# LSH attention feeding a domain mixture of experts: the softmax division moves behind the product with v

## The chip, the core and the metric

The kernel runs on one core of one Trainium2 chip. The metric is device microseconds (us) of one execution; three runs of the kernel before gave 774.47, 777.2 and 779.48 us, median 777.2.

The engines are named as the profile names them: PE (TensorE, matmuls and transposes; PEld is its weight load), DVE (VectorE), ACT (ScalarE), POOL (GpSimd) and SP, whose queue issues every DMA of this program. Each engine works through its own instructions in order; an instruction whose inputs are not there holds up all that stand behind it on that engine, and the same holds for the DMA issues in SP's queue.

## The reference

Two batches of eight heads, 768 positions, head size 64, everything in float32. Queries and keys are hashed by the signs of six projections; a query attends to the keys of its own bucket alone. The result, head by head side by side, goes through four experts weighted by given probabilities.

```
mask   = q_bucket[:, :, :, None] == k_bucket[:, :, None, :]
scores = where(mask, q @ k.T / sqrt(64), -1e9)
attn   = exp(scores - max(scores))
attn   = attn / (sum(attn) + 1e-9)
x      = attn @ v                      # (1536, 512) after heads are laid side by side
out    = sum over e of p[:, e] * (relu(x @ w1[e]) @ w2[e])   # w1 512x1024, w2 1024x512
```

## The kernel before, in words

float32 products are made of float32r parts: each operand is split into a rounded part and a remainder, and three products (high x high, high x low, low x high) are added up in PSUM. That is why so many tiles come as pairs: `pthi` and `ptlo`, `hh` and `hl`, `xhi` and `xlo`, `w1hi` and `w1lo`.

**Attention** is a loop over steps, one step for each tile of 128 queries: 2 x 8 heads x 6 tiles. Two tiles are a pair, in the code a group `g`. A tile goes through these stages, each some steps behind the first:

- S: scores on PE into `sps` (L337, L339), then on DVE the row minimum of the negated scores, copied out to `p` (L344).
- E: exp on ACT, in place, with the row sum in `den` (L360).
- M and N: on DVE `den` + 1e-9 (L493) and the reciprocal `rd` (L367); then POOL multiplies `p` by it, 128x768 for each tile (L370).
- T, for heads 0 to 8 of 16: PE transposes `p` into `ptps` (L386), ACT copies the rounded part to `pthi` (L390), DVE subtracts for `ptlo` (L391).
- X and H, for the seven last heads, which the code calls light: DVE transposes 32x32 blocks of `p` into `t` (L403); SP writes `t` to DRAM as `scr` (L407) and, when that has landed, reads it back in another order as `px` in four DMAs (L410). Two steps later ACT makes `pthi` of `px` (L424) and POOL `ptlo` (L425). There is one `px` buffer.
- V: PE multiplies with `vv`, first the `pthi` part, one step later the `ptlo` part (`pv`, L435); ACT and DVE add the two halves into `xf` (L452, L457, L464), and after an odd head POOL makes `xhi` and `xlo` of it (L468, L471).
- P: once a head, in its first three steps, the preparation of the next head: PE transposes, ACT and DVE split into `ah` and `al`, SP copies parts between partitions (`q<-ah` twice, `k<-ah`, then `ah<-al`), PE and ACT compute the hash signs, POOL turns them into mask rows (`al`, L279), SP copies those (`k<-al`, L287). The next head's second score matmul (L339) reads them. SP also loads q and k (`tqk`) and v (`tv`) for the head after the next.

The order of all this is written out by hand: in each step the stages are issued in the order of the string `ORDER`, and the constants `LAG_...` say how many steps after S a stage comes. An engine's instruction order is this issue order.

**Experts**: 16 units of 512 hidden columns (8 for each batch). A unit does 8 groups of 12 matmuls into a PSUM tile `mps` (L602 to L604), each followed by a relu `hh` on ACT (L609) and a remainder `hl` on DVE (L610), then 6 groups of 12 matmuls (L625 to L627), added into `acc` on DVE (L635). `mps`, `ptps` and `pv` share four PSUM buffers. The weights are loaded as `ws` (L566) and split on DVE and POOL (L577, L578).

Attention of batch 0 runs first. Then the experts of batch 0 run, with steps of attention of batch 1 put between their matmuls by a running count of estimated PE time, and last the experts of batch 1 alone.

Of the kernel before, what the change touches and what calls it, by code (L numbers as in the profile page):

```python
# [8 lines left out]
F32 = mybir.dt.float32  # L9
F32R = mybir.dt.float32r  # L10
ACTF = mybir.ActivationFunctionType
ALU = mybir.AluOpType
PSUM = bass.MemoryType.PSUM

P = 128
# [3 lines left out]
SGN_SCALE = float(2**20)  # L19
ATT_PACE = 1.04  # L20
LAG_E = 1
LAG_N = 2
LAG_T = 6
LAG_V = 7
PP_BUFS = 5
TW = 3
QK_AT = 1
XADD_POOL = 0
# [3 lines left out]
N_WARM = 16  # L32
WARM = (2, 4)
FIRST = 2
SPLIT_N = 1
W_STEP = 24
PREP_AT = 0
ORDER = "MTNXVSEP"
LIGHT_FROM = 9
LAG_VL = 8  # L40
DRAIN = 1000
LAG_X = 4
LAG_H = 6


@with_exitstack
def tile_lsh_attention__then__domain_moe(
# [11 lines left out]
    nc = tc.nc  # L59
    B, H, S, D = q.shape  # L60
    NB = proj.shape[1]
    E, DM, F = w1.shape
    NT = S // P
# [7 lines left out]
    G = 2  # L71
    GN = G * P
# [7 lines left out]
    const = ctx.enter_context(tc.tile_pool(name="const", bufs=1))  # L80
# [5 lines left out]
    dr = ctx.enter_context(tc.tile_pool(name="dr", bufs=2, space=bass.MemoryType.DRAM))  # L86
    ptp = ctx.enter_context(tc.tile_pool(name="ptp", bufs=2))
    sm = ctx.enter_context(tc.tile_pool(name="sm", bufs=6))
    xs = ctx.enter_context(tc.tile_pool(name="xs", bufs=2))
# [41 lines left out]
    def setup():  # L131
        nc.sync.dma_start(out=pr[0:D], in_=proj)
        nc.sync.dma_start(out=pr[D:P], in_=proj)
        nc.vector.memset(warm, 0.0)
        nc.scalar.activation(warm[:, 0:1], warm[:, 0:1], ACTF.Exp)
        make_identity(nc, ident)
        keep_warm(N_WARM)
        step_column(qk_scale, ((0, -scale), (D, 1.0)))
        step_column(
            sgn_bias, ((0, -TINY), (MQ + NB, TINY), (MQE, 0.0), (MK, TINY), (MK + NB, -TINY), (MKE, 0.0))  # L140
        )
        step_column(bit_mul, ((0, 0.5), (MK, BIG / 2)))
        nc.vector.memset(phi.bitcast(F32), 0.0)
        nc.vector.memset(plo.bitcast(F32), 0.0)
        for rows, m, sign in ((slice(0, D), MQ, -1.0), (slice(D, P), MK, -1.0)):
            sg = sign if m == MQ else sign
            for i, s in ((0, sg), (1, -sg)):
                cols = slice(m + i * NB, m + (i + 1) * NB)
                nc.vector.tensor_scalar(out=phi[rows, cols], in0=pr[rows], scalar1=s, scalar2=None, op0=ALU.mult)
                nc.vector.scalar_tensor_tensor(  # L150
                    out=plo[rows, cols],
                    in0=pr[rows],
                    scalar=s,
                    in1=phi[rows, cols].bitcast(F32),
                    op0=ALU.mult,
                    op1=ALU.subtract,
                )
# [152 lines left out]

    probs_t = {}
    dens = {}
    rds = {}
    pts = {}
    pvs = {}
    xf = {}
# [38 lines left out]
    def stage_e(b, h, t):  # L355
        pt, nb = probs_t[b, h, t]
        g, o = divmod(t, G)
        if o == 0:
            dens[b, h, g] = sm.tile([P, G], F32, tag="den", name="den")
        nc.scalar.activation(pt, pt, ACTF.Exp, bias=nb, scale=-1.0, accum_out=dens[b, h, g][:, o : o + 1])  # L360

    def stage_n(b, h, g):
        den = dens.pop((b, h, g))
        rd = sm.tile([P, G], F32, tag="rd", name="rd")
        if not SPLIT_N:
            nc.vector.tensor_scalar(out=den, in0=den, scalar1=1e-9, scalar2=None, op0=ALU.add)
        nc.vector.reciprocal(out=rd, in_=den)  # L367
        for o in range(G):
            pt, _ = probs_t[b, h, g * G + o]
            nc.gpsimd.tensor_scalar(  # L370
                out=pt, in0=pt, scalar1=rd[:, o : o + 1], scalar2=1.0, op0=ALU.mult, op1=ALU.mult
            )

    def stage_t(b, h, t):
        pt, _ = probs_t.pop((b, h, t))
# [53 lines left out]
    def stage_v(b, h, g, part):  # L429
# [16 lines left out]
        j, odd = divmod(h, 2)  # L446
        if not odd:
            xf[b, j, g] = xs.tile([P, GN], F32, tag=f"xf{g}", name="xf", bufs=1)
        x = xf[b, j, g]
# [6 lines left out]
        elif light(b, h):  # L456
            nc.vector.tensor_tensor(  # L457
                out=x[mine].rearrange("p (t a q) -> p a t q", t=G, q=32),
                in0=ps[mine, :GN].rearrange("p (a t q) -> p a t q", t=G, q=32),
                in1=tmp[mine].rearrange("p (a t q) -> p a t q", t=G, q=32),  # L460
                op=ALU.add,
# [2 lines left out]
            nc.vector.tensor_tensor(out=x[mine], in0=ps[mine, :GN], in1=tmp[mine], op=ALU.add)  # L464
        if odd:
            x = xf.pop((b, j, g))
            sl = slice(g * GN, (g + 1) * GN)
            nc.gpsimd.tensor_scalar(  # L468
                out=xhi[b, j][:, sl], in0=x, scalar1=1.0, scalar2=1.0, op0=ALU.mult, op1=ALU.mult
            )  # L470
            nc.gpsimd.tensor_tensor(  # L471
                out=xlo[b, j][:, sl], in0=x, in1=xhi[b, j][:, sl].bitcast(F32), op=ALU.subtract
            )
# [5 lines left out]
    def attention():  # L479
# [3 lines left out]
        def do(op, i):  # L483
            if op == "N":
                j = i - LAG_N
                if 0 <= j < n and j % G == G - 1:
                    b, h, t = seq[j]
                    stage_n(b, h, t // G)
            elif op == "M":
                j = i - LAG_N  # L490
                if SPLIT_N and 0 <= j < n and j % G == G - 1:
                    den = dens[seq[j][0], seq[j][1], seq[j][2] // G]
                    nc.vector.tensor_scalar(out=den, in0=den, scalar1=1e-9, scalar2=None, op0=ALU.add)  # L493
            elif op == "T":
                j = i - LAG_T
                if 0 <= j < n and not light(*seq[j][:2]):
# [219 lines left out]
```

## Time and profile before

| | |
|---|---|
| runs | 774.47, 777.2, 779.48 us |
| profiled execution, first to last instruction (span) | 779.2 us; the run of 779.48 us is the one that fits it, 0.3 us around the span |
| busy | PE 752.8 us (97%), DVE 459.4 (59%), POOL 401.8 (52%), ACT 279.0 (36%) |
| mean granted TensorE clock | 0.987 of full speed |
| chain that ended last | PE 69%, DMA 10%, DVE 8%, POOL 6%, ACT 3% |

Busy time is that of modelled matmul ends, so PE at 97% is not PE at its peak. The shares are means over stages that differ: in the page's 40 slices DVE and ACT are at nine tenths until about 140 us and at three or less behind 480 us. The chain that ended last holds, besides PE, the DMA `px<-scr` (4%), the DMA `scr<-t` (3%) and POOL's `ptlo` (3%).

### The profile page before, as it was taken

What the parts mean: (1) busy time and instruction counts of PE and PEld (TensorE: products, weight loads), DVE (VectorE), ACT (ScalarE), POOL (GpSimd) and SP (SyncE); (2) the same over time, 40 slices, a digit from 0 to 9 for tenths busy, and PEclk for the clock granted to TensorE, in tenths of its full rate; (3) what the DMA queues carried; (4) which work ended last, traced back from release to release, by engine and by line L of the source; (5) the groups of instructions that cost most, each with busy time, mean ns of one, the idle gap of its engine ahead of it and who ended that gap; (6) DMA issues with size and microseconds to landing.
All of it is one profiled execution on the core that took longest, in us unless ns stands there. A gap on an engine that the chain in (4) does not pass through costs nothing.

```text
span 779.2 us, 11435 instructions
## 1 busy us (share of the span) xinstructions
PE 752.8 (97%) x4186; PEld 690.4 (89%) x4186; DVE 459.4 (59%) x876; ACT 279.0 (36%) x556; POOL 401.8 (52%) x381
## 2 busy tenths in 40 slices
PE   7899999999989899999989989999999999999998
PEld 6789989898979888999888889898989989899896
DVE  4899999946758478565766734343443434524342
ACT  4899989641343433426244131110201102011020
POOL 1656686724579668667796855132251322414220
PEclk8999999999999999999999999999999999999999
DMA  3544535334657877676565733231121211113002
GB/s 91 144 111 110 117 85 131 74 87 140 181 154 199 226 186 217 177 202 179 156 209 162 200 111 95 80 124 55 55 81 37 100 51 59 55 54 109 28 27 82
DMA packets 67344, 92.29 MB, mean 118 GB/s; under 512 B 29860, under 2 KB 42660, under 8 KB 67288
## 3 DMA queue, kind: packets, MB, share of 16 engines
q1 hardware_dynamic: 67288, 91.56, 42.0%
q8 instruction: 33, 0.54, 0.3%
q14 instruction: 23, 0.19, 0.1%
HBM read 59.53 MB, written 19.66 MB: 102 GB/s over the span
## 4 chain that ended last, share of the span: by engine, by line
PE 69%; DMA 10%; DVE 8%; POOL 6%; ACT 3%; issue 2%; SPq 2%; POOLq 0%; ACTq 0%; DVEq 0%
PE mps L625 9%; PE mps L626 9%; PE mps L627 9%; PE mps L602 9%; PE mps L603 9%; PE mps L604 9%; PE pv L435 5%; DMA px<-scr 4%; DMA scr<-t 3%; PE ptps L386 3%; POOL ptlo L425 3%; PE sps L339 2%; PE sps L337 2%; DVE p L344 2%; DMA ah<-al 2%
## 5 line engine op out<-in xcount | busy, mean ns | idle before, releaser
L602 PE MATMUL mps<-xhi,w1hi 128*128 128x384 f32 x512 | 173.5, 339 | 5.8 <-DVE hl L610 5.8
L578 POOL TENSOR_TENSOR w1lo<-ws,w1hi 128x512 fp32r<-128x512 f32 x64 | 83.1, 1302 | 178.3 <-DVE w1hi L577 155.3
L604 PE MATMUL mps<-xhi,w1lo 128*128 128x384 f32 x512 | 172.9, 338 | 0.0
L603 PE MATMUL mps<-xlo,w1hi 128*128 128x384 f32 x512 | 172.9, 338 | 0.0
L609 ACT ACTIVATE hh<-mps 128x384 fp32r<-128x384 f32 x128 | 61.9, 490 | 301.1 <-PE mps L604 301.0
L610 DVE SCALAR_TENSOR_TENSOR hl<-mps,hh 128x384 fp32r<-128x384 f32 x128 | 70.4, 555 | 143.1 <-ACT hh L609 142.9
L625 PE MATMUL mps<-w2hi,hh 128*128 128x512 f32 x384 | 151.6, 395 | 0.4 <-DVE hl L610 0.4
L626 PE MATMUL mps<-w2lo,hh 128*128 128x512 f32 x384 | 150.9, 393 | 0.0
L627 PE MATMUL mps<-w2hi,hl 128*128 128x512 f32 x384 | 150.6, 392 | 0.0
L635 DVE SCALAR_TENSOR_TENSOR acc<-mps,pe,acc 128x512 f32<-128x512 f32 x84 | 62.9, 748 | 118.0 <-PE mps L627 118.0
L578 POOL TENSOR_TENSOR w2lo<-ws,w2hi 128x512 fp32r<-128x512 f32 x64 | 86.5, 1380 | 46.0 <-issue 37.8
L370 POOL TENSOR_SCALAR p<-p,rd 128x768 f32<-128x768 f32 x96 | 87.6, 924 | 32.1 <-DVE rd L367 28.6
L602 PEld LDWEIGHTS mps<-xhi,w1hi 128*128 128x128 f32 x512 | 97.0, 189 | 7.1 <-DVE hl L610 6.6
L603 PEld LDWEIGHTS mps<-xlo,w1hi 128*128 128x128 f32 x512 | 97.0, 189 | 0.4
L604 PEld LDWEIGHTS mps<-xhi,w1lo 128*128 128x128 f32 x512 | 97.2, 190 | 0.0
L344 DVE TENSOR_SCALAR_CACHE_REDUCE p<-sps 128x768 f32<-128x768 f32 x96 | 90.8, 947 | 4.6 <-PE sps L339 3.3
L360 ACT ACTIVATE p<-p,nb 128x768 f32<-128x768 f32 x96 | 89.6, 933 | 9.4 <-DVE p L344 8.2
L425 POOL TENSOR_TENSOR ptlo<-px,pthi 128x768 fp32r<-128x768 f32 x42 | 77.1, 1858 | 25.6 <-ACT pthi L424 21.4
L627 PEld LDWEIGHTS mps<-w2hi,hl 128*128 128x128 f32 x384 | 72.8, 190 | 15.7
L625 PEld LDWEIGHTS mps<-w2hi,hh 128*128 128x128 f32 x384 | 72.7, 189 | 14.6 <-DVE hl L610 0.6
L626 PEld LDWEIGHTS mps<-w2lo,hh 128*128 128x128 f32 x384 | 72.8, 190 | 13.8
L424 ACT ACTIVATE pthi<-px 128x768 fp32r<-128x768 f32 x42 | 33.2, 838 | 109.9 <-DMA px<-scr 109.9
(82 smaller groups left out, 953.2 us busy)
## 6 DMA issues: line engine op xcount, KB each, us to landing
ws<-in_moe_w_dram SPq DMA_DIRECT2D x64, 512.0 KB, 3.3
scr<-t SPq DMA_DIRECT2D x21, 768.0 KB, 4.3
px<-scr SPq DMA_DIRECT2D x84, 192.0 KB, 3.9
q<-ah SPq DMA_DIRECT2D x30, 192.0 KB, 3.2
tv<-in_v_dram SPq DMA_DIRECT2D x16, 192.0 KB, 3.6
out_dram<-acc SPq DMA_DIRECT2D x12, 256.0 KB, 2.5
tqk<-in_q_dram SPq DMA_DIRECT2D x15, 192.0 KB, 4.2
tqk<-in_k_dram SPq DMA_DIRECT2D x15, 192.0 KB, 3.8
```

Of the source, the lines that this page charges most:

```text
L344: nc.vector.tensor_scalar(out=two(pt), in0=ps[:, :, :NH], scalar1=MASKED, scalar2=MASKED, op0=ALU.min, op1=ALU.min, accum_out=nb,)
L360: nc.scalar.activation(pt, pt, ACTF.Exp, bias=nb, scale=-1.0, accum_out=dens[b, h, g][:, o : o + 1])
L370: nc.gpsimd.tensor_scalar(out=pt, in0=pt, scalar1=rd[:, o : o + 1], scalar2=1.0, op0=ALU.mult, op1=ALU.mult)
L425: nc.gpsimd.tensor_tensor(out=fl[:, sl], in0=px[:, sl], in1=fh[:, sl].bitcast(F32), op=ALU.subtract)
L578: nc.gpsimd.tensor_tensor(out=lo[:, c + o], in0=t[:, o], in1=hi[:, c + o].bitcast(F32), op=ALU.subtract)
L602: nc.tensor.matmul(ps[:, :SB], w1hi[:, kk, fs], xhi[b, kk][:, sl], start=kk == 0, stop=False)
L603: nc.tensor.matmul(ps[:, :SB], w1hi[:, kk, fs], xlo[b, kk][:, sl], start=False, stop=False)
L604: nc.tensor.matmul(ps[:, :SB], w1lo[:, kk, fs], xhi[b, kk][:, sl], start=False, stop=kk == KD - 1)
L610: nc.vector.scalar_tensor_tensor(out=hl, in0=ps[:, :SB], scalar=0.0, in1=hh.bitcast(F32), op0=ALU.max, op1=ALU.subtract)
L625: nc.tensor.matmul(ps, hh[:, ts], w2hi[:, f], start=f == 0, stop=False)
L626: nc.tensor.matmul(ps, hh[:, ts], w2lo[:, f], start=False, stop=False)
L627: nc.tensor.matmul(ps, hl[:, ts], w2hi[:, f], start=False, stop=f == FC - 1)
```

## The change

The probabilities are no longer divided before the product with v. The rows of x are, behind it:

- Gone: the epsilon add on DVE (L493, stage M) and POOL's two products of 128x768 a pair (L370).
- The epsilon is added on ACT (an Identity with a bias of 1e-9, 128x2, behind the second exp of a pair).
- Stage N: DVE takes the reciprocal into two columns of a standing tile of 128x32, and transposes that tile in 32x32 blocks into `rt`. SP writes two DMAs of 4x32 from it, one for each tile, to a small DRAM row `row` of 2x128.
- A new stage R, one step later: SP reads `row` back, broadcast over the 64 partitions of the head's half, into `rdb`.
- When both heads of a pair of heads are in `xf`, POOL multiplies it by `rdb`, 128x256, ahead of `xhi` and `xlo`.
- All lags are shorter: T from 6 to 4 steps, V from 7 to 6 (light heads 8 to 7), X from 4 to 3, H from 6 to 5; N goes from 2 to 3. There are four `p` buffers in place of five. The order within a step is `TXVSENRP` in place of `MTNXVSEP`. Because the lags change by odd numbers, X, H and N now fall into the even steps, in which the preparation issues `q<-ah`, `k<-ah` or `k<-al`; before they fell into the odd ones, with `ah<-al` and the loads of q and k.

```diff
-LAG_N = 2
-LAG_T = 6
-LAG_V = 7
-PP_BUFS = 5
+LAG_N = 3
+LAG_R = 4
+LAG_T = 4
+LAG_V = 6
+PP_BUFS = 4
...
-ORDER = "MTNXVSEP"
+ORDER = "TXVSENRP"
 LIGHT_FROM = 9
-LAG_VL = 8
+LAG_VL = 7
 DRAIN = 1000
-LAG_X = 4
-LAG_H = 6
+LAG_X = 3
+LAG_H = 5
...
-    rds = {}
+    rds = [const.tile([P, 32], F32, name=f"rd{i}") for i in range(2)]
+    for t in rds:
+        nc.vector.memset(t, 1.0)
...
         nc.scalar.activation(pt, pt, ACTF.Exp, bias=nb, scale=-1.0, accum_out=dens[b, h, g][:, o : o + 1])
+        if o == G - 1:
+            den = dens[b, h, g]
+            nc.scalar.activation(den, den, ACTF.Identity, bias=eps)
...
     def stage_n(b, h, g):
         den = dens.pop((b, h, g))
-        rd = sm.tile([P, G], F32, tag="rd", name="rd")
-        if not SPLIT_N:
-            nc.vector.tensor_scalar(out=den, in0=den, scalar1=1e-9, scalar2=None, op0=ALU.add)
-        nc.vector.reciprocal(out=rd, in_=den)
+        rd = rds[(h * NT // G + g) % 2]
+        nc.vector.reciprocal(out=rd[:, 0:G], in_=den)
+        rt = sm.tile([P, 32], F32, tag="rt", name="rt", bufs=2)
+        nc.vector.transpose(out=rt, in_=rd)
+        rows[b, h, g] = dr.tile([G, P], F32, tag="row", name="row", bufs=6)
         for o in range(G):
-            pt, _ = probs_t[b, h, g * G + o]
-            nc.gpsimd.tensor_scalar(
-                out=pt, in0=pt, scalar1=rd[:, o : o + 1], scalar2=1.0, op0=ALU.mult, op1=ALU.mult
-            )
+            nc.sync.dma_start(out=rows[b, h, g][o].rearrange("(r q) -> r q", q=32), in_=rt[o:P:32])
+
+    def stage_r(b, h, g):
+        j, odd = divmod(h, 2)
+        if not odd:
+            rdbs[b, j, g] = xs.tile([P, GN], F32, tag=f"rdb{g}", name="rdb", bufs=1)
+        row = rows.pop((b, h, g))
+        nc.sync.dma_start(
+            out=rdbs[b, j, g][odd * D : (odd + 1) * D],
+            in_=row.rearrange("g p -> (g p)").partition_broadcast(D),
+        )
...
         if odd:
             x = xf.pop((b, j, g))
+            nc.gpsimd.tensor_tensor(out=x, in0=x, in1=rdbs.pop((b, j, g)), op=ALU.mult)
```

How the instructions stand, first SP's queue in the attention of batch 0, the issues of one head before (names are out<-in; the brackets list the semaphores waited for, DMAHW being earlier DMAs):

```order
L265 DMA q_1081<-ah 64x768 [waits Activation_49]
L266 DMA q_1081<-ah 64x768
L267 DMA k_1084<-ah 64x768 [waits DMAHW0_49,PE_49]
L274 DMA ah<-al 64x768 [waits DMAHW6_49,DMAHW1_49,DMAHW7_49,DVE_49,PE_49]
L180 DMA tqk<-in_q_dram 128x6x64 [waits DMAHW2_49]
L180 DMA tqk<-in_k_dram 128x6x64 [waits DMAHW3_49]
L287 DMA k_1084<-al 12x768 [waits DMAHW4_49,Pool_49]
L187 DMA tv<-in_v_dram 128x384 [waits DMAHW5_49,Pool_49]
```

These eight are all there is. The same place of the change, from the first preparation DMA of a head to its third pair of `row` writes:

```order
L267 DMA q_915<-ah 64x768 [waits DMAHW5_49,Activation_49]
L268 DMA q_915<-ah 64x768 [waits DMAHW6_49]
L269 DMA k_918<-ah 64x768 [waits PE_49]
L387 DMA rdb<-row 64x256 [waits DMAHW4_49,DMAHW3_49]
L276 DMA ah<-al 64x768 [waits DMAHW5_49,DMAHW1_49,DMAHW6_49,DVE_49,PE_49]
L182 DMA tqk<-in_q_dram 128x6x64 [waits DMAHW2_49]
L182 DMA tqk<-in_k_dram 128x6x64
L380 DMA row<-rt 4x32 [waits DVE_49]
L380 DMA row<-rt 4x32
L289 DMA k_918<-al 12x768 [waits Pool_49]
L387 DMA rdb<-row 64x256 [waits DMAHW7_49,DMAHW5_49,DMAHW4_49]
L380 DMA row<-rt 4x32 [waits DVE_49]
```

Between each pair of `row` writes and the `rdb` that waits for both stand the preparation's issues of that even step: three, one, and one (`tv`).

Next, SP's queue beside the experts, where a light head is in work. Before, from the end of one `px` to the next pair's:

```order
L410 DMA px<-scr 32x4x384 [waits DMAHW5_49]
L274 DMA ah<-al 64x768 [waits DMAHW6_49,PE_49]
L180 DMA tqk<-in_q_dram 128x6x64 [waits DMAHW7_49]
L180 DMA tqk<-in_k_dram 128x6x64 [waits DMAHW0_49]
L566 DMA ws<-in_moe_w_dram 128x2x512 [waits Pool_49]
L287 DMA k_3588<-al 12x768 [waits DMAHW2_49,Pool_49]
L407 DMA scr<-t_3763 128x1536 [waits DMAHW3_49,DVE_49]
L410 DMA px<-scr 32x4x384 [waits DMAHW4_49,DMAHW5_49,DMAHW3_49,Pool_49]
```

and the same preparation DMAs in the change:

```order
L276 DMA ah<-al 64x768 [waits DMAHW6_49,DMAHW2_49,DMAHW7_49,DVE_49,PE_49]
L182 DMA tqk<-in_q_dram 128x6x64 [waits DMAHW3_49]
L182 DMA tqk<-in_k_dram 128x6x64
L425 DMA scr<-t_3048 128x1536 [waits DVE_49]
L428 DMA px<-scr 32x4x384 [waits DMAHW5_49,Pool_49]
L428 DMA px<-scr 32x4x384
L428 DMA px<-scr 32x4x384 [waits DMAHW0_49]
L428 DMA px<-scr 32x4x384 [waits DMAHW1_49]
L380 DMA row<-rt 4x32 [waits DMAHW2_49,DVE_49]
L380 DMA row<-rt 4x32 [waits DMAHW3_49]
L289 DMA k_2955<-al 12x768 [waits DMAHW4_49,Pool_49]
L387 DMA rdb<-row 64x256 [waits DMAHW3_49,DMAHW2_49]
```

Before, `ah<-al` stood behind the four `px`, and `k<-al` directly ahead of the next `scr`; now `ah<-al` stands ahead of `scr`, and `k<-al` behind `px`, with an `rdb` between it and the next `scr`.

Last, DVE in the attention of batch 0, one pair of steps before:

```order
L344 TENSOR_SCALAR p_408,nb<-sps 128x768 [waits PE_49]
L493 TENSOR_SCALAR den<-den 128x2 [waits Activation_49]
L391 TENSOR_TENSOR ptlo<-ptps,pthi 128x3x128 [waits Activation_49] x2
L367 RECIPROCAL rd<-den 128x2 [waits DVE_49]
L464 TENSOR_TENSOR xf<-pv,xtmp 64x256 [waits Activation_49]
L344 TENSOR_SCALAR p,nb<-sps 128x768 [waits PE_49,Pool_49]
L391 TENSOR_TENSOR ptlo<-ptps,pthi 128x3x128 [waits Activation_49] x2
```

and in the change:

```order
L348 TENSOR_SCALAR p_650,nb<-sps 128x768 [waits PE_49]
L409 TENSOR_TENSOR ptlo<-ptps,pthi 128x3x128 [waits PE_49,Activation_49]
L409 TENSOR_TENSOR ptlo<-ptps,pthi 128x3x128 [waits Activation_49]
L482 TENSOR_TENSOR xf<-pv,xtmp 64x256 [waits Activation_49]
L348 TENSOR_SCALAR p_749,nb<-sps 128x768 [waits PE_49]
L375 RECIPROCAL rd_134<-den 128x2
L377 STREAM_TRANSPOSE rt<-rd_134 128x32 [waits DMAHW7_49,DMAHW6_49,DVE_49]
L409 TENSOR_TENSOR ptlo<-ptps,pthi 128x3x128 [waits Activation_49] x2
```

The add is gone and its wait for ACT with it; the transpose stands directly behind the reciprocal that it waits for, and also waits for the `row` writes of two pairs before. The first `ptlo` of a pair of tiles now waits for PE as well: its buffer is the one that `pv` of two pairs before reads, and that `pv` is issued in the same step behind the transposes.

## Rows read from the trace of the kernel before

**Rows 1.** Stretches: us, busy us (instructions) of each engine, clock, DMA share, GB/s.
```profile
60.00:80.00 20.00, 20.00 (x151) 19.35 (x150) 19.02 (x49) 18.86 (x42) 13.01 (x17) 1.00 0.45 105
```
**Rows 2.** Waits of PE, stretches 180:280 and 396:456 us: total, times, longest.
```profile
PE tps L257 <- DVE p L344: 2.6, 1, 2.6
PE pv L435 <- DVE hl L610: 2.3, 1, 2.3
PE mps L602 <- DVE hl L610: 4.9, 2, 2.8
```
**Rows 3.** Waits over the whole span, and SP's own: total, times, longest.
```profile
ACT pthi L424 <- DMA px<-scr: 109.9, 20, 10.0
PE ptps L386 <- POOL p L370: 2.1, 2, 1.1
SPq L410 <- DMA scr<-t: 87.8, 21, 7.2
```
**Rows 4.** Timeline 246:276 us: start, us, engine, line, instruction [idle before, releaser].
```profile
252.95 1.84 DVE L403 STREAM_TRANSPOSE t<-p 128x768 f32<-128x768 f32 x2
256.63 0.91 POOL L279 TENSOR_SCALAR al<-k,bit_mul 44x768 fp32r<-44x768 f32 x1 [3.83 <-DMA ah<-al]
257.57 0.84 SPq L287 DMA_DIRECT2D k<-al  x1
258.51 0.45 SPq L407 DMA_DIRECT2D scr<-t  x1
269.62 1.58 ACT L424 ACTIVATE pthi<-px 128x768 fp32r<-128x768 f32 x2 [7.42 <-DMA px<-scr]
```
**Rows 5.** Stretches of 4 us behind two of PE's stalls (clock third from the end).
```profile
220.00:224.00 4.00, 4.00 (x14) 3.15 (x13) 3.90 (x10) 1.97 (x5) 4.00 (x4) 0.59 0.49 198
404.00:408.00 4.00, 4.00 (x15) 4.00 (x16) 3.06 (x7) 1.56 (x5) 3.92 (x4) 0.57 0.78 290
```
**Rows 6.** Groups by line, whole span: count, busy us, mean ns, idle before.
```profile
L370 POOL TENSOR_SCALAR p<-p,rd 128x768 f32<-128x768 f32 x96 | 87.6, 924 | 32.1 <-DVE rd L367 28.6 <-ACT p L360 2.1
L471 POOL TENSOR_TENSOR xlo<-xf,xhi 128x256 fp32r<-128x256 f32 x24 | 18.0, 751 | 2.0
```
**Rows 7.** Timeline 10:34 us, the first steps.
```profile
22.20 0.90 SPq L287 DMA_DIRECT2D k<-al  x1
23.23 0.88 PE L386 MATMUL ptps<-ident,p 128*128 128x128 f32 x6 [1.09 <-POOL p L370]
24.63 0.62 PE L339 MATMUL sps<-k,al 76*128 76x384 f32 x2 [0.17 <-DMA k<-al]
```
**Rows 8.** Timeline 58:76 us, attention of batch 0 in full swing.
```profile
61.78 0.96 PE L435 MATMUL pv<-ptlo,vv 128*128 128x256 f32 x6
61.99 0.19 ACT L360 ACTIVATION_READ_ACCUMULATOR p<-p,nb 128x1 f32 x1
62.08 0.85 ACT L390 ACTIVATE pthi<-ptps 128x384 fp32r<-128x384 f32 x2
62.65 1.02 DVE L391 TENSOR_TENSOR ptlo<-ptps,pthi 128x384 fp32r<-128x384 f32 x2
```
**Rows 9.** Groups by line in 58.02:133.06 us, five heads (hps to hps).
```profile
L493 DVE TENSOR_SCALAR den<-den 128x2 f32<-128x2 f32 x15 | 3.7, 249 | 0.0
L367 DVE RECIPROCAL rd<-den 128x2 f32<-128x2 f32 x15 | 2.3, 153 | 0.0
L452 ACT ACTIVATE xtmp<-pv 64x256 f32<-64x256 f32 x15 | 5.7, 379 | 1.1 <-PE pv L435 0.7
```
**Rows 10.** Timeline of SP, 0:148 us: three of one head's eight issues.
```profile
71.34 0.53 SPq L265 DMA_DIRECT2D q<-ah  x1
...
79.01 0.82 SPq L287 DMA_DIRECT2D k<-al  x1
83.67 0.34 SPq L187 DMA_DIRECT2D tv<-in_v_dram  x1
```
**Rows 11.** Timeline of PE, 80:90 us: the next head's first score matmuls.
```profile
84.22 0.52 PE L339 MATMUL sps<-k,al 76*128 76x384 f32 x2
```

More of the change, by code (lines that the diff above doesn't have):

```diff
@@ L34 @@
 FIRST = 2
-SPLIT_N = 1
 W_STEP = 24
 PREP_AT = 0
-ORDER = "MTNXVSEP"
+ORDER = "TXVSENRP"
 LIGHT_FROM = 9
-LAG_VL = 8
+LAG_VL = 7
 DRAIN = 1000
-LAG_X = 4
-LAG_H = 6
+LAG_X = 3
+LAG_H = 5
 @with_exitstack
@@ L110, in tile_lsh_attention__then__domain_moe @@
     plo = const.tile([P, MKE], F32R, name="plo")
+    eps = const.tile([P, 1], F32, name="eps")
     warm = const.tile([P, 8], F32, name="warm")
@@ L134, in setup @@
         nc.vector.memset(warm, 0.0)
+        nc.vector.memset(eps, 1e-9)
         nc.scalar.activation(warm[:, 0:1], warm[:, 0:1], ACTF.Exp)
@@ L360, in stage_e @@
         nc.scalar.activation(pt, pt, ACTF.Exp, bias=nb, scale=-1.0, accum_out=dens[b, h, g][:, o : o + 1])
+        if o == G - 1:
+            den = dens[b, h, g]
+            nc.scalar.activation(den, den, ACTF.Identity, bias=eps)
+    rdbs = {}
+    rows = {}
     def stage_n(b, h, g):
         den = dens.pop((b, h, g))
-        rd = sm.tile([P, G], F32, tag="rd", name="rd")
-        if not SPLIT_N:
-            nc.vector.tensor_scalar(out=den, in0=den, scalar1=1e-9, scalar2=None, op0=ALU.add)
-        nc.vector.reciprocal(out=rd, in_=den)
-        for o in range(G):
-            pt, _ = probs_t[b, h, g * G + o]
-            nc.gpsimd.tensor_scalar(
-                out=pt, in0=pt, scalar1=rd[:, o : o + 1], scalar2=1.0, op0=ALU.mult, op1=ALU.mult
-            )
+        rd = rds[(h * NT // G + g) % 2]
[3 more added lines that the diff above has]
+        rows[b, h, g] = dr.tile([G, P], F32, tag="row", name="row", bufs=6)
+        for o in range(G):
+            nc.sync.dma_start(out=rows[b, h, g][o].rearrange("(r q) -> r q", q=32), in_=rt[o:P:32])
[8 more added lines that the diff above has]
+        )
     def stage_t(b, h, t):
@@ L488, in do @@
                     stage_n(b, h, t // G)
[L489 to L493, printed above, removed]
+            elif op == "R":
+                j = i - LAG_R
+                if 0 <= j < n and j % G == G - 1:
+                    b, h, t = seq[j]
+                    stage_r(b, h, t // G)
             elif op == "T":
```

## The prediction

> **What bounds the kernel now.** Three stages: the page's slices show attention of batch 0 alone to about 150 us (A), the mixture of experts of batch 0 with attention of batch 1 between its matmuls to about 475 us (B), and experts alone (C). C does not change. In A the table of stretches shows three engines close to full at once: of 20 us PE is busy 20.00, DVE 19.02, ACT 18.86, POOL 13.01 [rows 1]. Work taken from POOL helps A only where someone waits for POOL; work given to DVE or ACT has about 1 us in 20 to hide in.
>
> In B, PE is the bound, and what is lost is its stalls. The list of waits names them: PE stood still 2.6, 2.3 and twice together 4.9 us, mostly behind `hl` on DVE [rows 2]. Those four are one mechanism. ACT waits in order for `px`, the transposed probabilities on their way back from DRAM: 109.9 us, 20 times, 10.0 at most [rows 3]. Behind it on ACT stands `hh`, the relu that frees the experts' PSUM, so a long wait stops PE. The row at 269.62 is such a wait of 7.42 us [rows 4]. Each stall may also cost clock: the stretches behind two of them show granted clocks of 0.59 and 0.57 over 4 us [rows 5], part of it at the lower level of 1.2 GHz, that is 0.41 x 4 = 1.6 and 0.43 x 4 = 1.7 us. With a third like them: 2.6 + 2.3 + 4.9 = 9.8 us idle and 5.0 us of clock, 14.8 in all, 3.7 a stall.
>
> Why `px` was late there [rows 4]: DVE's transposes `t` ended at 252.95 + 1.84 = 254.79, but SP issued `scr` at 258.51. Before it in SP's queue stood `k<-al` (257.57), which waited for POOL's `al` (256.63), which waited 3.83 us for the DMA `ah<-al`, whose issue SP had held behind the `px` of the pair before.
>
> **The change, part by part.**
>
> *Division on POOL.* 96 instructions of 924 ns go, 87.6 us; 24 products of 128x256 come, at most the 751 ns of the two-input `xlo` of that shape, 18.0 us [rows 6]. POOL is hidden except where PE waited for it: 2.1 us in two waits [rows 3], one of 1.1 at 23.23 [rows 7]. That one belongs to the next item; the other gives -1.0 (0 if DVE or ACT ends last there).
>
> *Shorter lags.* Transposes T start two steps earlier. At the start PE must wait until 24.63 for the second head's `k` [rows 7], unchanged; two T of 0.88 now fit ahead of that. Between 0 and -1.8; I take -1.3, as PE has little else to do there.
>
> *ACT.* The epsilon becomes an Identity of 128x2, 24 of them in A. Not in the trace; the nearest row is the accumulator read, 0.19 us at 61.99, with the next instruction at 62.08 [rows 8]. Identity needs what the read writes, so it starts at 62.18, and the next one some 0.25 us later than now. The far bounds: 0.1 (only a slot) and 0.38 (the 64x256 `xtmp` [rows 9]). 24 x 0.25 = 6.0 us of ACT (2.4 to 9.1). Cover is ACT's idle 1.14 in 20, or 0.86 a head of 15.0 us (75.04 / 5 in the stretch of [rows 9]), against 0.75 needed. Without cover it is +6; I charge +1.5. The Trainium skill (ScalarE: Activation LUTs, Rules for kernel authors) wants additions on VectorE and budgets about 0.3 us for an ACTIVATE; by that estimate it is 24 x 0.3 = 7.2 us of ACT instead of 6.0 and a charge nearer +2; no run here shows this instruction yet.
>
> *DVE.* The epsilon add goes (0.249 us in A, some of it waiting), a transpose of 128x32 comes behind the reciprocal and waits for it [rows 9]. Price between 0.04 (a 24th of the 0.92 us that one 128x768 takes [rows 4]) and 0.25; nearest in size is the reciprocal, 0.153. Net -0.1 to +0.1 a pair, -2.4 to +2.4 in A; I take +0.5. The order of instructions adds a wait: the first `ptlo` of a pair now waits for the `pv` of two pairs before, issued in the same step. Its cover: PE starts that `pv` at 61.78 and it ends by 62.74; DVE begins at 62.65 anyway [rows 8]. Price 0, with 0.2 x 24 = 4.8 if DVE ever runs closer behind PE.
>
> *SP, stage A.* A head has eight issues between 71.34 and 83.67, 0.34 to 0.82 us, 4.6 in all [rows 10]. Nine come: six `row` writes and three `rdb` reads. Between 0.34 and 0.82 each: 3.1 to 7.4. `rdb` waits in the queue until its `row` has landed; the nearest landing is `k<-al`, issued 22.20 and needed at 24.63, 2.43 us [rows 7]. Between them lie three issues, one, and one, so the waits are at most some 0.7 + 1.6 + 2.1 = 4.4 a head. Total 7.7 to 16.4 of 15.0 us; I take 14.0: nine issues of 0.55, as that of q at 71.34, and the waits whole. Behind them in the queue is `k<-al`: issued 79.01, landed 81.4, wanted by the next head's `sps` at 84.22 [rows 10, 11], so 2.8 us of cover. Price 0.
>
> *SP and POOL, stage B.* X moves to the even steps, so `scr` stands behind `rdb`, no longer behind `k<-al`; `ah<-al` and the loads of q and k go out in the odd step, no longer behind the wait for `scr` nor beside `px` in flight; POOL's `ptlo`, whose end releases the `px` buffer, has no division ahead of it (2 x 0.92). I expect three of the four stalls gone: -11.1. Against it stand three more issues a pair in a queue that waits 87.8 / 21 = 4.2 us for each `scr` [rows 3]: half a new stall, +1.8. Net -9.3, bounds -14.8 and +3.7.
>
> Sum: -1.0 - 1.3 + 1.5 + 0.5 - 9.3 = -9.6. The span is 779.2; the run of 779.48 would be its own time with 0.3 around it. 779.5 - 9.6 = 769.9 for such an execution; the median of the three runs, 777.2, lies 2.3 below it, so **768**.
>
> **Rivals.**
>
> *The stalls stay (0.20).* For: from the issue of `scr` at 258.51 to `pthi` at 269.62 are 11.1 us of transfers [rows 4], and none gets faster; X and H are still two steps apart. Against: 3.7 of the 7.4 us in the traced case came from the queue. Time: 777.2 - 2.3 + 2.0 = 777.
>
> *ACT and DVE set the pace of A (0.10).* For: three engines at 94% or more. Against: PE's own groups already fill the stretch. +6.0 and +2.4 uncovered: 777.2 - 2.3 - 9.3 + 8.4 = 774.
>
> *SP sets the pace of A, slower (0.16).* It decides once the three new issues of a pair with their waits pass (15.0 - 4.6) / 3 = 3.5 us; then `k<-al` is late for every head and PE waits at `sps`. At 0.82 an issue and 1.6 of waiting a pair is 4.1, a head 16.8, and seven heads lose 1.8 each: +12.6; with no gain in B: 777.2 - 2.3 + 12.6 = 788. For: the slowest issue, 0.82, is the one with few partitions, and a `row` has four. Against: the eight issues of a head do not wait for each other's landing, 4.6 us of queue for transfers of 2.4 us and more each. The Trainium skill (DMA: Bandwidth & Descriptors, Rules for kernel authors) speaks for this rival: small transfers should be joined, since under 64 KB they are mostly overhead, and a `row` is 512 bytes. By that rule this is the case that comes; the trace bears it out for `k<-al`, 36 KB with 2.43 us, but not for how many are in flight at once.
>
> **Numbers.** Forecast case 0.46, 758 to 772, of it 0.36 under the bound. All stalls gone and A gaining too: 0.08, about 756. A change of 1%, 7.8 us, is about what a measurement here tells from none. Faster (under 769.4): 0.36 + 0.08 + 0.01 of the ACT case = 0.45. Same: 0.10 + 0.18 + 0.09 = 0.37. Slower: 0.16 + 0.02 of the staying stalls = 0.18. Range 756 to 788, with about 0.06 left out below and 0.09 above; the forecast's own range is 758 to 772.
>
> **What would show it.** Right: ACT's total wait for `px` well below 109.9, at most two PE stalls over 2 us in B, clock slices of B without dips, POOL near 332 us busy, the first head's T near 20 us. ACT in A at 19.5 of 20 with PE waiting behind `pthi` would show the ACT case; PE waiting at `sps` for the DMA `k<-al` at each head, and `row` issues near 0.8 us, the SP case; `px` waits of 6 us again, the staying stalls. I am wrong in the main step if B ends no earlier relative to A than now.

## The result and the profile after

The changed kernel takes **780.9 us** (median of 20 runs, 778.3 to 786.5) against 777.2 (20 runs of the kernel before on the same chip, 773.6 to 782.6): a ratio of **1.0055 [1.0038, 1.0072]**, slower by 0.5%, where 768 was forecast. An execution's time is its span plus 1.7 us here (778.26 for the profiled span of 776.5), not plus 0.3 as the prediction took it; the traced execution of before (span 779.2) is one of about 780.9 us, and none of the three runs listed with it.

That profiled span is the shortest of the 20, while the traced execution of before lies above its median. So the two traces show which stage lost and which gained, but not by how much the ends differ. A second trace of each, taken later, lies on the same sides (779.4 and 777.5).

As in the prediction, A is the attention of batch 0 alone and B the experts of batch 0 with the attention of batch 1 between their matmuls. The first two fences are the changed kernel's page (busy time of each engine) and its stretch that answers to [rows 1], with the same columns.

```profile
PE 751.0 (97%) x4186; PEld 686.6 (88%) x4186; DVE 451.9 (58%) x879; ACT 292.5 (38%) x604; POOL 334.8 (43%) x309
```
```profile
60.00:80.00 20.00, 19.15 (x136) 17.46 (x135) 17.18 (x42) 17.46 (x39) 4.03 (x5) 1.00 0.47 112
```

POOL lost what it should (401.8 to 334.8 us). But in A no engine is fuller than before; PE, DVE and ACT all fell by 0.9 to 1.8 us in 20. They wait for one another. How far that slows A is read from the first matmul of each head's `hps`, the hash product of the preparation, and from the first expert matmul. Here are the rows of these two tiles, `hps` from 20 us on (earlier ones start at 15.6 and 14.7), in the kernel before and then in the changed one (count, shortest/median/longest ns, first and last start):

```profile
L273 PE MATMUL hps<-ah,phi x16: 332/380/430, 28.0 to 133.3; 128*108 128x384 f32 x16
...
L602 PE MATMUL mps<-xhi,w1hi x512: 331/334/522, 148.9 to 758.4; 128*128 128x384 f32 x171
```
```profile
L275 PE MATMUL hps<-ah,phi x16: 332/336/429, 28.4 to 141.8; 128*108 128x384 f32 x16
...
L621 PE MATMUL mps<-xhi,w1hi x512: 332/334/446, 154.1 to 755.7; 128*128 128x384 f32 x171
```

Seven heads take 113.4 us in place of 105.3, **16.2 us a head for 15.0**. The experts start 5.2 us later, though A now holds less work: one step of `sps` and one group of `tps` less, one group of `ptps` more. From such a group's start to PE's next instruction is 0.71, 0.66 and 0.58 us (medians before, 60 to 140 us; 0.79 for a group of `pv`), so that is 0.8 us less, and for equal work A lost **6.0**. Most of it lies behind the `hps` at 28 us: from there to the first expert matmul are 125.6 us with one group of each of the four less (2.7 us), against 120.8, so 7.5 lost. Ahead of it 1.5 are gained: `hps` comes 0.4 later, but two groups of `ptps` and one of `pv` more are done by then.

The last expert matmul of the first layer starts 2.7 us earlier all the same, so from A's end on the traced executions differ by -2.7 - 6.0 = -8.7, and the second pair of traces by -8.2. By the medians it is less: 777.2 - 1.7 - 148.9 = 626.6 before, 780.9 - 1.7 - 154.1 - 0.8 = 624.3 now, **-2.3**. This takes A's end from the traces, where it moves little: 148.9 and 149.2 before, 154.1 and 154.7 now, and up to 1.8 us away in other runs with the same A. The runs of one kernel spread by 8 to 9 us; that this arises in B is likely, but no trace of a fast and a slow run of one kernel shows it.

The waits of PE in 180:480 us of the changed kernel, which answer to [rows 2], and in the same window of the second trace of before (total, times, longest):

```profile
PE sps L341 <- DVE p L348: 4.5, 3, 2.7
PE mps L621 <- DVE hl L629: 2.6, 3, 1.0
PE pv L453 <- DVE hl L629: 1.4, 1, 1.4
PE mps L644 <- DVE hl L629: 0.7, 2, 0.4
```
```profile
PE mps L602 <- DVE hl L610: 6.6, 4, 2.8
PE pv L435 <- DVE hl L610: 5.0, 3, 2.1
PE tps L257 <- DVE p L344: 2.2, 1, 2.2
PE mps L625 <- DVE hl L610: 0.4, 1, 0.4
```

One stall of over 2 us is left of four or five. ACT still waits 92.6 us for `px` (109.9 before [rows 3]).

Where A loses is seen behind a head's `hps`. The timeline of 93:97 us in the changed kernel, columns as in [rows 4]:

```profile
93.07 0.60 PE L275 MATMUL hps<-ah,phi 128*108 128x384 f32 x2 [0.26 <-DVE al L264]
...
93.86 0.95 DVE L348 TENSOR_SCALAR_CACHE_REDUCE p<-sps 128x768 f32<-128x768 f32 x1
...
94.45 0.90 ACT L277 ACTIVATE k<-hps,sgn_bias 44x768 fp32r<-44x768 f32 x1 [1.45 <-POOL w1lo L597]
...
95.38 0.87 ACT L408 ACTIVATE pthi<-ptps 128x384 fp32r<-128x384 f32 x2
...
95.90 1.02 DVE L409 TENSOR_TENSOR ptlo<-ptps,pthi 128x384 fp32r<-128x384 f32 x2 [1.08 <-ACT pthi L408]
...
96.84 0.41 DVE L482 TENSOR_TENSOR xf<-pv,xtmp 64x256 f32<-64x256 f32 x1
...
97.17 0.94 DVE L348 TENSOR_SCALAR_CACHE_REDUCE p<-sps 128x768 f32<-128x768 f32 x1
```

ACT stands still until `hps` is there, then does `k`, then `pthi`, and DVE waits 1.08 us for it. Such a wait comes once a head (0.75 to 1.41 us in five heads). `xf` comes only behind it and pushes DVE's next row minimum (`min`, L348) out. The same place in the kernel before:

```profile
87.51 0.60 PE L273 MATMUL hps<-ah,phi 128*108 128x384 f32 x2
...
88.90 0.43 DVE L464 TENSOR_TENSOR xf<-pv,xtmp 64x256 f32<-64x256 f32 x1
89.36 0.96 DVE L344 TENSOR_SCALAR_CACHE_REDUCE p<-sps 128x768 f32<-128x768 f32 x1
...
90.35 1.02 DVE L391 TENSOR_TENSOR ptlo<-ptps,pthi 128x384 fp32r<-128x384 f32 x2
```

There `ptlo` comes as late behind `hps` (2.84 us, 2.83 in the change), but `xf` and `min` fill the time ahead of it. With LAG_V 6 the end of a product, `xtmp` and `xf`, falls on the even steps, and the step with `hps` is odd; with LAG_V 7, before, it fell on the odd ones, so that `xf` filled that gap. The mean interval between the two `min` around this wait is 3.48 us in the changed kernel and 2.30 before (six heads). Part of that is only moved: the interval ahead of it, which `xf` has left, is shorter by 0.35 (3.23 for 3.58). The two together lose 0.8 of the 1.2 us a head.

The wait that the prediction named is there too: one that the line of `ptlo` before (L391) has not, an instruction of 21 ns in the view of the line L409:

```profile
L409 DVE TENSOR_TENSOR ptlo<-ptps,pthi x108: 515/548/559, 19.8 to 182.2; 128x384 fp32r<-128x384 f32 x108
L409 DVEq EVENT_SEMAPHORE  x25: 21/21/21, 31.1 to 174.8; - x25
```

In 9 of 15 places between 60 and 138 us that `ptlo` starts 0.10 to 0.12 us behind the end of the `pv` that reads its buffer (in one, 84.07 against 83.96), and not 0.1 us behind DVE's instruction before it: there it costs about 0.1 us a pair. At the wait behind `hps` it stands hidden: that `pv` ends at 95.74, 0.16 us ahead of `ptlo`, so an earlier `pthi` alone would not have let DVE go on much sooner.

The new instructions themselves are as small as thought (groups by line in five heads, 60.60:141.50 us):

```profile
L367 ACT ACTIVATE den<-den,eps 128x2 f32<-128x2 f32 x15 | 4.4, 296 | 0.5
L377 DVE STREAM_TRANSPOSE rt<-rd 128x32 f32<-128x32 f32 x15 | 3.2, 212 | 0.5
```

### The profile page after: what moved, and what is told of

Read it like the earlier page. It is cut to its first block, busy times and chain, and to the rows that moved or that the text cites. A ratio compares the mean times of both kernels' runs of the same rounds, so it can differ in the third digit from the quotient of the medians.

```text
span 776.5 us, 11484 instructions
## 1 busy us (share of the span) xinstructions
PE 751.0 (97%) x4186; PEld 686.6 (88%) x4186; DVE 451.9 (58%) x879; ACT 292.5 (38%) x604; POOL 334.8 (43%) x309
## 4 chain that ended last, share of the span: by engine, by line
PE 61%; DMA 13%; DVE 10%; ACT 5%; issue 4%; POOL 3%; SPq 3%; DVEq 0%; ACTq 0%; POOLq 0%
PE mps L621 9%; PE mps L644 9%; PE mps L646 9%; PE mps L645 9%; PE mps L623 9%; PE mps L622 9%; DMA px<-scr 5%; DMA scr<-t 5%; DVE p L348 3%; PE pv L453 3%; DVE ptlo L409 3%; SPq L428 2%; ACT pthi L442 2%; PE sps L343 1%; DMA q<-ah 1%
## 5 line engine op out<-in xcount | busy, mean ns | idle before, releaser
L348 DVE TENSOR_SCALAR_CACHE_REDUCE p<-sps 128x768 f32<-128x768 f32 x96 | 91.0, 948 | 4.4 <-PE sps L343 4.0
L646 PEld LDWEIGHTS mps<-w2hi,hl 128*128 128x128 f32 x384 | 72.0, 188 | 15.4
L442 ACT ACTIVATE pthi<-px 128x768 fp32r<-128x768 f32 x42 | 33.2, 839 | 92.6 <-DMA px<-scr 92.6
L409 DVE TENSOR_TENSOR ptlo<-ptps,pthi 128x384 fp32r<-128x384 f32 x108 | 54.5, 546 | 11.8 <-ACT pthi L408 9.8
```

Of the source, the lines that this page charges most:

```text
L348: nc.vector.tensor_scalar(out=two(pt), in0=ps[:, :, :NH], scalar1=MASKED, scalar2=MASKED, op0=ALU.min, op1=ALU.min, accum_out=nb,)
L409: nc.vector.tensor_tensor(out=ol, in0=src, in1=oh.bitcast(F32), op=ALU.subtract)
L646: nc.tensor.matmul(ps, hl[:, ts], w2hi[:, f], start=False, stop=f == FC - 1)
```

## The experiments

"Pace" is the mean time from one head's `hps` to the next over six heads, from the second on: 15.1 us in the kernel before, 16.3 in the changed one. Ratios are to runs of the kernel before on the same chip.

### What slows A

**Without the Identity.**
```
-        if o == G - 1:
-            nc.scalar.activation(den, den, ACTF.Identity, bias=eps)
```


> The changed kernel without the Identity on ScalarE (the epsilon of 1e-9 is left out of the denominators). Theory Z1: the Identity, 0.30 us after each pair's second accumulator read, sets the slower pace of stage A (16.15 us a head against 15.00). Then the pace falls by 3 x 0.30 = 0.9 to about 15.2 us and the time from 781 by 7 x 0.9 = 6.3 to about 774.5. Theory Z2: the new lags do it (the transposes stand too close behind the softmax, PE waits for the ptlo that frees a PSUM buffer): pace stays 16.1, time 780 to 781. Theory Z3: the row and rdb transfers on SP do it: pace stays, 780 to 781.


Measured: 780.0, ratio 1.0026 [1.0007, 1.0046]; pace 16.2. Z1 falls: the Identity is a small part of A's loss.

**Without row and rdb.**
```
-            nc.sync.dma_start(out=rows[b, h, g][o]..., in_=rt[o:P:32])
...
-        nc.sync.dma_start(out=rdbs[b, j, g]..., in_=row...)
...
+        rdbs[b, j, g] = ones
```


> The changed kernel without the six row writes and three rdb reads of a head (the product after pv takes a tile of ones, so the softmax division is left out; reciprocal and 128x32 transpose stay). Z3: the pace of stage A falls from 16.15 to about 15.0 us a head and the time by up to 8 to 773; in stage B the SP queue is shorter as well, up to 2 us more. Z1 and Z2: pace 16.1, time 778 to 781.


Measured: 780.05, 1.0044 [1.0018, 1.0070]; pace 16.2. Z3 falls: nine more issues a head cost A next to nothing.

**Old distances of T and V.** `LAG_T = 4, LAG_V = 6` to `6, 7`.


> The changed kernel with the transposes and the product of batch 0 and the first head of batch 1 back at the old distances (LAG_T 6, LAG_V 7 in place of 4 and 6); everything else, the lags of the later heads too, as changed. Z2: the pace of stage A goes back to about 15.0 us a head; 8 us less there, 1.3 given back at the start: about 774. Z1 and Z3: pace 16.1, time 781 to 783.


Measured: 780.7, 1.0038 [1.0017, 1.0059]. The rows of this kernel:

```profile
L275 PE MATMUL hps<-ah,phi x16: 332/380/431, 26.7 to 134.3; 128*108 128x384 f32 x16
...
L621 PE MATMUL mps<-xhi,w1hi x512: 332/334/443, 148.6 to 759.0; 128*128 128x384 f32 x171
```

The pace is 15.4, and from the `hps` near 27 us to the first expert are 121.9 us with the same PE work as before (120.8; in the changed kernel 125.6 and 2.7 of work left out): 6.5 of 7.5 us are back, although Identity, transpose and rows are all there. Z2 holds in that the lags do it; no run moved T alone. The interval behind `hps` is 2.48 again, and the semaphore row of L409 is gone. Its timeline there:

```profile
88.33 0.60 PE L275 MATMUL hps<-ah,phi 128*108 128x384 f32 x2 [0.35 <-DVE al L264]
...
89.56 0.43 DVE L482 TENSOR_TENSOR xf<-pv,xtmp 64x256 f32<-64x256 f32 x1
...
90.65 0.87 ACT L408 ACTIVATE pthi<-ptps 128x384 fp32r<-128x384 f32 x2
...
91.17 1.02 DVE L409 TENSOR_TENSOR ptlo<-ptps,pthi 128x384 fp32r<-128x384 f32 x2 [0.19 <-ACT pthi L408]
```

`pthi` and `ptlo` come as late behind `hps` as in the changed kernel (2.8 us), but `xf` is done by then. The end, though, has not moved: what A gained, B gave back.

**Short lags without the change.** In the kernel before: `LAG_T 6, V 7, VL 8, X 4, H 6`, five buffers, to `4, 6, 7, 3, 5` and four.


> The kernel before (division on POOL ahead of the transposes) with the lags of the change and its 4 instead of 5 probability buffers (LAG_T 4, LAG_V 6, LAG_VL 7, LAG_X 3, LAG_H 5). Z2: the pace of stage A is 16 us a head or more, since the division now stands between exp and the transposes as well: 781 or more. Z1 and Z3: the pace stays near 15.0 to 15.3; if the other parity of X and H is what stage B gained by (some 4 us on the mean of the runs), the time is about 773; if the division on POOL was, about 777.


Measured: 837.1, 1.080 [1.0745, 1.0854]; a head takes 21.5 us (34.39 to 184.82), and PE waits for POOL's division:

```profile
PE ptps L386 <- POOL p L370: 47.6, 26, 4.2
```

The direction was that of Z2, the size far above it (Z2 asked for 16 us a head or more): the short lags are only to be had because the division left this path. What the fifth buffer is worth in it no run tells.

**V one step earlier.** `LAG_V = 6` to `5`.


> The changed kernel with the product of the first nine heads one step earlier (LAG_V 5 for 6), so that the second half of a pv (the reader of ptlo) stands a step ahead of the transposes that write the same ptlo buffer again. Theory Z4: stage A lost its time because the first ptlo of each pair waits for the pv that was issued in the same step; in the trace it starts 0.10 to 0.17 us behind the end of that pv in 13 of 16 pairs, with DVE idle up to 1.4 us before. Then the pace of A goes from 16.15 to about 15.3 us a head and the experts start near 147 us; the time is about 775 if stage B keeps what it has. Theory Z6: B gives the gain back, as in the run with the old distances, because its stalls depend on how the steps of attention fall between the matmuls: A faster by 5 to 6, time 779 to 782.


Measured: 781.3, 1.0039 [1.0012, 1.0066]. Here, too, the semaphore row of L409 is gone, and the interval behind `hps` is 2.47; but the last steps of a head are 0.1 to 0.25 us slower each than with the old distances, and the pace is 15.85, not 15.3. Z4 is half right: one step of LAG_V removes 0.4 of the 0.9 us a head that both distances give back. This edit removes the wait for `pv` and puts `xf` on the odd steps at once, as the old distances do; the rows above speak for the second as the larger part, but no run does the one without the other. Again the end did not move.

**Reciprocal and transpose one step later.** `LAG_N = 3, LAG_R = 4` to `4, 5`.


> The changed kernel with reciprocal, 128x32 transpose and row writes one step later (LAG_N 4, LAG_R 5 for 3 and 4); the wait of ptlo for pv stays. Theory Z5, a rival of Z4: what slows A is that reciprocal and transpose fall on the same step as the xf of the product, so that DVE's steps are uneven (2.8 and 2.0 us). Then the pace of A falls to about 15.4 us a head, the time to about 776. Z4: the pace stays at 16.0 to 16.2 and the time near 780.


Measured: 782.0, 1.0041 [1.0012, 1.0070]; pace 16.2, the interval behind `hps` 3.51. Z5 falls as put: it is not the reciprocal's step that matters. For that of `xf` speak the runs with the old distances and with V 5.

### Why the end does not follow A

**Only the lags of the later heads, in the kernel before.** `LAG_X 4, H 6, VL 8` to `3, 5, 7`.


> The kernel before with the lags of the later heads from the change (LAG_X 3, LAG_H 5, LAG_VL 7); the division stays on POOL ahead of them, stage A stays as before. If the other parity of X and H in the queues is what makes stage B of the changed kernel shorter (some 3 to 6 us), the time is 772 to 774. If the division's leaving POOL is, the time stays at 777, or rises, since the transposes t now stand one step closer behind the division.


Measured: 781.9, 1.0018 [0.9989, 1.0046]. ACT's wait for `px` in 150:480 falls from 109.9 to 60.0 us and the time does not: that total is no measure of PE's stalls, though the prediction took it for one.

**Another pace of attention in B.** `ATT_PACE = 1.04` to `1.00`.


> The changed kernel with attention of batch 1 spread a little thinner between the experts' matmuls (ATT_PACE 1.00 for 1.04); no instruction is added or removed, stage A is the same. Z6 (stalls of B depend on how the steps fall): B moves by 3 us or more in either direction, 776 or 785. Otherwise B's length is a matter of the work in it: 780 to 782.


Measured: 782.8, 1.0049 [1.0023, 1.0075]; no difference to the changed kernel's ratio. A miss for Z6.

**V 5 and one more step in A.** `for _ in range(3): next(att)` ahead of the experts.


> The run with LAG_V 5 in which, between stage A and the experts, one more step of attention is issued (three calls: sps, transposes and a pv), so that the first X of the later heads again stands four steps behind the first expert, as in the changed kernel and in the kernel before; with LAG_V 5 it stood five, in the run with the old distances three. Theory Z6: B's extra loss in those two runs came from this shift. Then the experts start near 151 us, B is as long as in the changed kernel and what A gained stays: about 777. Rival: B takes back whatever A gains, by what the work in it is: 781.


Measured: 785.7, 1.0115 [1.0076, 1.0154], the other way. The steps at which X stands are not what counts. **The same without the Identity:**


> As the run before it, and without the Identity on ScalarE (the epsilon of 1e-9 is left out). By Z6 about 776, and A's pace a little under 15.6 us a head, since ACT's 0.30 us a pair is one of the things that a DVE ptlo can wait for; by its rival 780 to 781.


Measured: 783.8, 1.0090 [1.0063, 1.0118]; no better.

**Second traces of both kernels.**


> The kernel before once more, for a second trace of stage B: the first trace (span 779.2) lay 3 us above the median of its runs. Expected: A ends at 148 to 150 us as in the first; PE's stalls in B between 9 and 13 us, and fewer stretches with a lowered granted clock than the four of the first trace.

> The changed kernel once more, for a second trace of stage B: the first (span 776.5) lay 3 us below the median of its runs. Expected: A ends at 153 to 156 us as in the first; stalls in B near 9 to 12 us, and one or two stretches with a lowered granted clock, of which the first trace had none.


Measured: spans 779.4 and 777.5; A's ends 149.2 and 154.7; PE idle in B 14.2 and 8.0 us (12.9 and 9.3 in the first traces). The granted clock was lowered in three slices of 4 us (0.57, 0.58, 0.59) and in one (0.57), which took about 5.0 and 1.7 us of B; in the first traces four such slices took 6.8 and none 0. Each of them begins at the end of one of PE's stalls of 2 us or more or within 2 us of it, but for one in the first trace of before (305 us). A's ends are as expected; the idle times lie a little outside (9 to 13 and 9 to 12).

Then the order of PE's instructions was set beside that of the changed kernel, counting expert matmuls from the first. Where A ends one step later or earlier, nearly every `sps` and `pv` of batch 1 stands in another place: one PSUM group of 12 expert matmuls (4 us) earlier in the run with the old distances, in the run with only the later heads' lags and in the runs with one more step, one or two groups later with V 5 alone. In the run with N 4, which had the changed kernel's stall, all are in the same places. With the other pace of attention most stand one to three groups later, which cost nothing. The next runs move only that.

**Places alone.** `da = 0.0` to `da = -654 * (b == 0)`, in the changed kernel.


> The changed kernel, with attention of batch 1 given a start of 654 cost units (a third of a step), so that nearly all its matmuls stand one group of 12 expert matmuls earlier in PE's order, where they stand in the run with LAG_V 5 and one step more in A and in the run with the old distances; no instruction is added or removed, A is the same. Theory Z7 (the placement in B sets its length): B shows those runs' stalls (mps waiting 3.6 to 4 us for hl between 230 and 280, 3 to 5 us between 430 and 480) and is 6 to 7 us longer: 786 to 788. Rival (B takes back what A gains, wherever attention is placed): 780 to 782.


Measured: 787.3, 1.0099 [1.0073, 1.0125]; the experts start at 155.1. By the median Z7 to the letter, by the ratios 0.4%. PE's waits in 155:480:

```profile
PE mps L644 <- DVE hl L629: 7.7, 3, 5.8
PE mps L621 <- DVE hl L629: 5.2, 3, 3.2
PE mps L623 <- POOL w1lo L597: 1.0, 1, 1.0
```

The longest, in this kernel's timeline, and the same pair of tiles in the changed kernel:

```profile
260.86 1.15 SPq L585 DMA_DIRECT2D ws<-in_moe_w_dram  x2
262.05 0.47 SPq L425 DMA_DIRECT2D scr<-t  x1
270.90 1.75 SPq L428 DMA_DIRECT2D px<-scr  x4
276.34 1.58 ACT L442 ACTIVATE pthi<-px 128x768 fp32r<-128x768 f32 x2 [10.90 <-DMA px<-scr]
278.94 0.80 PE L644 MATMUL mps<-w2hi,hh 128*128 128x512 f32 x1 [5.75 <-DVE hl L629]
```
```profile
257.57 0.37 SPq L585 DMA_DIRECT2D ws<-in_moe_w_dram  x1
260.60 0.73 SPq L425 DMA_DIRECT2D scr<-t  x1
265.75 2.56 SPq L428 DMA_DIRECT2D px<-scr  x4
271.89 1.58 ACT L442 ACTIVATE pthi<-px 128x768 fp32r<-128x768 f32 x2 [5.55 <-DMA px<-scr]
```

DVE's `hl` behind this wait holds PE for 5.75 us. From the issue of `scr` to that of `px` are 8.9 us with two weight loads issued 1.2 us ahead of it, and 5.2 with one load 3.0 ahead. That the loads are the reason is argued from these rows, not tried.

**The fast A in the changed kernel's places.** `LAG_T 6, LAG_V 7` and `da = 654 * (b == 0)`.


> The run with the old distances of transposes and product (LAG_T 6, LAG_V 7), whose experts start near 148.6 us, with attention of batch 1 held back by 654 cost units, so that from its seventh step on all its matmuls stand in the changed kernel's places. Z7: A's gain of 5 to 7 us now stays: 774 to 776, faster than the kernel before by a little. Rival: 780 to 781 as without it.


Measured: **775.4**, 0.9969 [0.9947, 0.9990], where without the 654 it was 1.0038. A's gain now reaches the end; Z7 holds. **Without the Identity too:**


> The run with the old distances held back by 654 units, and without the Identity on ScalarE (the epsilon of 1e-9 left out), the best version that the runs so far point to. Z7: 773 to 775, below both kernels. Rival: 779 to 781.


Measured: 775.8, 0.9970 [0.9950, 0.9989], the same; Identity costs the end nothing.

**V 5 in those places.** `LAG_V = 5` and `da = -1306 * (b == 0)`.


> The run with LAG_V 5, whose experts start near 148 us, with attention of batch 1 given a start of 1306 units, which puts its matmuls into the changed kernel's places from its seventh step on. Its A gained 4 us for equal work. Z7: 776 to 778. Rival: 780 to 782.


Measured: 780.4, 1.0032 [1.0004, 1.0060]. A miss: the places are a large part, not the whole.

**The division back on POOL, with the later heads' lags and the places of the fast A.** The kernel before with `LAG_X 3, H 5, VL 7` and `da = 654 * (b == 0)`.


> The kernel before with the changed kernel's lags of the later heads (LAG_X 3, LAG_H 5, LAG_VL 7) and attention of batch 1 held back by 654 units: its matmuls then stand in the same places as in f2_old_t_v_placed, stage A is that of the kernel before, and the division stays on POOL ahead of X. If the division's leaving POOL is worth something in B, this is slower than f2's 775.4: 778 or more. If placement and the lags of X and H are all of B's gain, it is 774 to 776.


Measured: 781.4, 1.0050 [1.0023, 1.0076]; PE's waits in 155:480:

```profile
PE pv L435 <- DVE hl L610: 5.5, 1, 5.5
PE mps L602 <- DVE hl L610: 4.3, 4, 2.8
PE mps L625 <- DVE acc L631: 3.5, 1, 3.5
```

The places are those of the run at 775.4. Between the two lie 0.8% (6.3 us), to the credit of the division's leaving POOL, with what else differs (step order, buffers, Identity, rows). Their mean granted clocks differ as well, 0.987 and 0.9955 (medians of 12 runs each), which is 6.6 us of 777. In the places one group earlier the same difference was worth nothing (1.0018 with the division, 1.0038 without).

**The kernel before, places alone.** `da = 654 * (b == 0)`.


> The kernel before, with attention of batch 1 held back by 654 units and nothing else: its matmuls stand one group of 12 later than before, between the places of the two kernels. Z7 (places set B's length) lets B move by 2 us or more, in a direction that no run tells yet: 774 or 780. Rival (before's places are as good as any): 776.5 to 778.


Measured: **772.8**, 0.9936 [0.9907, 0.9964], the fastest of all, with none of the change in it. So the 6.3 us hold only beside the short lags of the later heads; with the old ones the lowest time of all has the division in it. The row of this kernel:

```profile
L602 PE MATMUL mps<-xhi,w1hi x512: 331/334/522, 147.1 to 749.2; 128*128 128x384 f32 x171
```

## Why the prediction was wrong

**POOL (-1.0), and start (-1.3).** POOL's 334.8 us are the forecast 332. PE's wait for the division is gone, but waits for `ptlo` stand in its place. The first transposes start at 17.9 us, where they started at 23.2, and by equal work the `hps` near 28 us is reached 1.5 us earlier, near the forecast. But that point moves by 1.4 us between executions with the same A (26.7 and 28.1 with the old distances), as much as the term, so the start is not told from chance.

**ACT (+1.5).** The Identity takes 0.296 us. The estimate of 0.3 us from the Trainium skill (ScalarE: Activation LUTs, Rules for kernel authors) agrees with this row. Leaving it out gains 0.6 us (in the changed kernel) or 1.3 (between the two kernels with the fast A and the changed kernel's places) in seven heads: the charge was high enough.

**DVE (+0.5), and the order that makes `ptlo` wait for `pv` (0): the step that failed in A.** The prediction saw that V had come into another step, looked only at the wait for the `ptlo` buffer there, and priced it at nothing by a cover read from one row [rows 8]. That wait is small where it shows, about 0.1 us a pair. What it missed in the same edit is that V by one step changes its parity: `xtmp` and `xf` leave the steps in which ACT waits for `hps` and join those with the reciprocal and transpose. DVE, with 19.0 of 20 us busy before, then idles about 1 us a head and has its work afterwards. The lags of T and V priced at nothing cost the most of A's 7.5 us: put back, they return 6.5, and without the Identity too, from the `hps` near 27 us to the first expert are 120.8 us, as before. That it is the parity of `xf` in these lags is read from the timelines and from the interval behind `hps` in both runs that move it back, which also lose the wait for `pv`. Of the 0.9 us a head that the old distances give back, 0.5 can be followed to that place (the two intervals, 3.23 + 3.48 = 6.71 us, are 3.74 + 2.48 = 6.22 there); the rest lies in the other steps. The rival "ACT and DVE set the pace of A" had the right stage and size (+8.4), by another cause: its instructions were there in the run with the old distances, too, and A was fast.

**SP in A (0).** Right: without all nine transfers the pace is 16.2 for 16.3. By the Trainium skill (DMA: Bandwidth & Descriptors, Rules for kernel authors) small transfers should be joined, since under 64 KB they are mostly overhead. What they cost is not waited for here, and the rival that SP sets the pace is out.

**B (-9.3): the term that was mis-sized.** In the two pairs of traces B is 8.7 and 8.2 us shorter, with three or four of the long stalls gone and granted clock won, as the steps said. By the medians it is 2.3, about the size of the granted clock alone (0.993 in the 20 runs of the changed kernel, 0.990 to 0.991 in the sets of runs of before; 0.002 to 0.003 of 778 us are 1.6 to 2.3): the term was sized on the stalls of one execution that lies above its median. And the cause is not the queue alone. The change with the old distances of T and V, against the kernel before with the same places and the short lags of the later heads, is worth 6.3 us or nothing; places alone are worth 3 to 6 in either kernel. Each held back by 654 units, the kernel before (0.9936) is ahead of the change with the old distances (0.9969), though the intervals overlap. The prediction did not look at where the attention steps fall between the expert matmuls, which the change moves because it changes the step at which A ends.

Sum: A +6.0 in place of -0.3 (with the start in it), B -2.3 in place of -9.3: +3.7, the measured difference. Both misses are of one size, 6.3 and 7.0 us; A's turned the sign. What stays open is what the other steps of a head lose, why the last steps of a head are slower with V 5, why that kernel gained little in the good places, and what in a place makes the stalls.

## What to carry to other kernels

Where a change moves a step by some slots, write out each engine's steps anew, with what shares a step with what: a lag changed by an odd number moves work out of gaps that it filled, and a cover read from the old order no longer holds. Where one stream is dealt out between another's matmuls, a stage before it that ends a step earlier also shifts the dealing, and this can be worth more than the change: move the offset alone, in both kernels, before a gain or loss is put down to the work removed. And a term sized on the stalls of one traced execution needs that execution's place among its runs.

## What the runs showed of the hardware

A small ACT instruction of 128x2 takes 0.296 us, where one of 64x256 takes 0.379; a DVE transpose of 128x32 takes 0.212, where one of 128x768 takes 0.92. The `scr` write of 768 KB was followed by the issue that waits for it after 5.2 us in one place and 8.9 in another.
